# Halves of K stored by token and head, halves of P stored by head: the order of the fp16 stationary operands in SBUF

## The chip, the cores and the metric

The kernel runs on one core of a Trainium2 chip. The metric is the device time of one execution in microseconds; lower is better. Of three runs of the kernel before, the median is 1122.11 us (1119.1 to 1122.72). The profile comes from one further execution.

## The reference

Three stages follow one another in one launch, on 4 batches × 768 tokens with 8 heads of 48.

```python
# 1. delta-rule attention: a 48x48 state for each batch and head, 768 tokens in sequence
k_n = k / (np.linalg.norm(k, axis=-1, keepdims=True) + 1e-06)
for t in range(S):
    y[:, :, t] = np.einsum('bhd,bhde->bhe', q[:, :, t], state)
    v_old = np.einsum('bhde,bhd->bhe', state, kt)
    state = state + bt[:, :, :, None] * np.einsum('bhd,bhe->bhde', kt, vt - v_old)
# 2. mixture of 8 experts (384 -> 1024 -> 384), each token goes to the expert of its largest gate logit
h = np.maximum(x[mask] @ w1[e], 0.0)
out[mask] = gate_w[mask, None] * eom[mask, e, None] * (h @ w2[e])
# 3. gated layer on all 3072 tokens (384 -> 1536 -> 384)
gate = 1.0 / (1.0 + np.exp(-(x @ w_gate)))
return (gate * (x @ w_val)) @ w_out
```

## The kernel before, in words

**Attention.** The 768 tokens are cut into 24 chunks of 32 (`NSTEP`). The recurrence within a chunk is solved at once: a triangular 32×32 system for every batch and head is inverted on VectorE ahead of time, for groups of four chunks. The 4 batches stand in four strips of 32 tokens on the 128 partitions; two batches share the 128 columns of a state matmul. The loop `for s in range(NSTEP)` does one chunk a pass. Its PE stream, in order, with the names that the profile shows:

- `KS`: the keys times the state (fp32). VectorE makes `W` from it: the values less what the state already holds.
- `Y` from `QB`: the queries times the state (fp32).
- `U`: the inverted system `TBD` times `W` (fp32). ScalarE rounds the result to fp16, `UH[:, 0]`, and VectorE stores what is left over as `UH[:, 1]`.
- `XTP`, and later `GL`: the gate of the mixture for the chunk before; then six of eight heads of `GP`, the key-key and key-query products of the chunk 11 ahead, which feed the inverse (`G`) and the masked query-key weights (`P`).
- `Sps` from `KBD`: the state's update. For each half p of the partitions (two batches), three passes over eight heads, 48 matmuls: hi·hi, lo·hi, hi·lo (`PASS`). The stationary operand is `KBD`, 64 rows × 128 columns, and the moving one is `UH`, 48 columns. ScalarE copies the sums to `SH`, with which the next chunk's `KS` starts.
- `Y` from `PBD`: the output within the chunk, 24 matmuls, 128 rows × 128 columns stationary, 48 columns moving.
- `GL`, then the other two heads of `GP`.

`KBD` and `PBD` hold fp16 halves: the upper half is the value rounded to fp16, the lower half the rest, rounded. They are block-diagonal by batch: where a strip's rows meet another batch's columns there are zeros, written once at the start. Each has two buffers, used in turn for pairs of chunks (u = s // 2).

**How K's halves arise.** The raw keys of a pair of chunks are loaded token by token, in the order (d, h) in a row (`load_kth`). ScalarE scales them head by head by the inverse norm (`kh_mul`), then casts them to fp16 (`kh_split_hi`). GpSimd forms the lower half (`kh_split_lo`). Four DMAs on the SP queue (`kexp`) write the strips into `KBD`. In `KBD` a row holds, for each of its two batches, 64 places for d with the 8 heads innermost, so a head's 128 columns are every eighth element.

**How P's halves arise.** `gp_evac` takes the `GP` products out of PSUM with two ScalarE copies, `G` as it lies and `P` turned from (h, i) to (i, h), i being the query's token. GpSimd scales and masks it (`p_split`), ScalarE casts the upper half (`p_split_hi`), GpSimd forms the lower (`p_split_lo`), and four DMAs on the SP queue (`expand`) write the strips into `PBD`. There a row holds, for four batches, 32 tokens with 16 (chunk, head) places innermost, so that a matmul's 128 columns are every sixteenth element. For the first four chunks `p_first` and `p_evac` do the same with a scaled ScalarE copy for each head.

**What sets the order.** Every engine of the attention issues in the order in which the code is written (`Queue` chains each instruction to the one before on its engine). The `Filler` puts the operations of the inverse between VectorE's main ones by a budget of estimated times, when the program is built. So the order doesn't follow measured times. Matmuls on zeros (`zf`, named by the tile they write) fill places where PE would wait.

Ahead of the loop, the first loads, the first inverse and the products of chunks 0 to 11 are made. The experts (lines around 1093 and 1130) and the gated layer (lines 1419 and 1445) follow the loop; during its last four passes the first expert weights are loaded and split.

Of the kernel before, what the change touches and what calls it, by code (L numbers as in the profile page):

```python
# [7 lines left out]
F32 = mybir.dt.float32  # L8
F32R = mybir.dt.float32r
F16 = mybir.dt.float16  # L10
I32 = mybir.dt.int32
U32 = mybir.dt.uint32
AF = mybir.ActivationFunctionType
ALU = mybir.AluOpType
# [134 lines left out]
class Attention:  # L149
# [5 lines left out]
    def run(self, small, acc, zero_fill, small_loads):  # L155
        tc, a, beside = self.tc, self.a, self.beside
        nc = tc.nc
        V, A, G = [Queue(tc, e) for e in (nc.vector, nc.scalar, nc.gpsimd)]
        T, SP = Queue(tc, nc.tensor), Queue(tc, nc.sync)
        engines = (V, A, G, T, SP)  # L160
        ctx, early = ExitStack(), ExitStack()
        wk = ctx.enter_context(tc.tile_pool(name="at_w", bufs=1, side="right"))
        cp = ctx.enter_context(tc.tile_pool(name="at_c", bufs=1, side="right"))
# [9 lines left out]
        rnt = cp.tile([128, NG, 32], F32, name="rnt")  # L173
        nt = cp.tile([128, NG, 32], F32, name="nt")
        mask = cp.tile([128, 32], F32, name="mask")
# [2 lines left out]
        KB = [(ep if i < 8 else cp).tile([128, 2, 64, 8], F32, name=f"KB{i}") for i in range(RK)]  # L178
        QB = [cp.tile([128, 2, 64, 8], F32, name=f"QB{i}") for i in range(2)]
        TBD = [(cp if i else ep).tile([128, 2, 1024], F32, name=f"TBD{i}") for i in range(2)]  # L180
        PBD = [cp.tile([128, 2, 4, 512], F16, name=f"PBD{i}") for i in range(2)]
        KBD = [cp.tile([128, 2, 2, 2, 64, 8], F16, name=f"KBD{i}") for i in range(2)]
        Sps = [pp.tile([128, 512], F32, name=f"Sps{i}") for i in range(2)]
        KT, VT, KTOK, KHG, GPM, PHL, LT = {}, {}, {}, {}, {}, {}, {}

# [19 lines left out]
        def load_v(u):  # L205
            t = wk.tile([128, 2, 384], F32, tag="VT", name="VT", bufs=2)
            SP.dma_start(out=t, in_=a["vtok"][:, 2 * u : 2 * u + 2])
            VT[u] = t
# [36 lines left out]
        QF, PM, PP = {}, {}, {}  # L245
# [6 lines left out]
        def p_first(s):  # L252

            u, s2 = divmod(s, 2)
            q = QF[s]
            if s2 == 0:
                PM[u] = wk.tile([128, 32, 16], F32, tag="PHL", name="PM", bufs=4)
            tag = ("GP", "XTP", "GL", "U")[s]
            ps = pool(tag).tile([128, 8, 64], F32, tag=tag, name="P0", bufs=1)
            for h in range(8):  # L260
                for p in range(2):
                    T.matmul(out=ps[64 * p : 64 * p + 64, h, 0:32], lhsT=KB[s][0:112, p, :, h], rhs=q[0:112, p, :, h], start=True, stop=True)
            PP[s] = ps

        def p_evac(s):
            u, s2 = divmod(s, 2)
            ps = PP.pop(s)
            for h in range(8):
                A.activation(out=PM[u][:, :, 8 * s2 + h], in_=ps[:, h, 0:32], func=AF.Copy, scale=rnt[:, 0, 8 * s + h : 8 * s + h + 1])

        def gp_evac(s):

            ps = GPS.pop(s)
            KT.pop(s)
            g, s4 = divmod(s, 4)
            if s4 == 0 and g > 0:
                GPM[g] = [ep.tile([128, 32, 32], F32, tag=n, name=n, bufs=b) for n, b in (("G", 2), ("P", 2))]
            A.copy(out=GPM[g][0][:, 8 * s4 : 8 * s4 + 8], in_=ps[:, :, 0:32])
            return A.copy(out=GPM[g][1][:, :, 8 * s4 : 8 * s4 + 8].rearrange("p i h -> p h i"), in_=ps[:, :, 32:64]).ins


        PMS = {}
# [1 line left out]
        def p_split(u):  # L284
            g, i = divmod(u, 2)
            if g:
                pm = GPM[g][1][:, :, 16 * i : 16 * i + 16]
                G.tensor_tensor(out=pm, in0=pm, in1=rnt[:, g, 16 * i : 16 * i + 16].unsqueeze(1).to_broadcast([128, 32, 16]), op=ALU.mult)
            else:
                pm = PM.pop(u)  # L290
            G.tensor_tensor(out=pm, in0=pm, in1=mask.unsqueeze(2).to_broadcast([128, 32, 16]), op=ALU.mult)
            PHL[u] = wk.tile([128, 2, 32, 16], F16, tag="PHL", name="PHL", bufs=4)
            PMS[u] = pm

        def p_split_hi(u):
# [4 lines left out]

        def expand(dst, src):
            for b in range(4):
                SP.dma_start(out=dst[32 * b : 32 * b + 32, :, b], in_=src[32 * b : 32 * b + 32].rearrange("p a i k -> p a (i k)"))


        def kh_mul(u, half=None):
            r = rnt[:, u // 2].rearrange("p (s h) -> p s h", s=4)
            for i in (range(2) if half is None else (half,)):
                kt = KTOK[u][:, i]
                if u == 0 or KA:  # L310
                    for h in range(8):
                        A.activation(out=kt[:, :, h], in_=kt[:, :, h], func=AF.Copy, scale=r[:, 2 * (u % 2) + i, h : h + 1])
                    continue
                G.tensor_tensor(out=kt, in0=kt, in1=r[:, 2 * (u % 2) + i].unsqueeze(1).to_broadcast([128, 48, 8]), op=ALU.mult)

        def kh_split_hi(u):
            KH = wk.tile([128, 2, 2, 384], F16, tag="KH", name="KH", bufs=1)
            src = KTOK[u].rearrange("p s d h -> p s (d h)")
            for s in range(2):
                A.copy(out=KH[:, s, 0], in_=src[:, s])  # L320
            KHG[u] = KH

        def kh_split_lo(u):
            KH = KHG[u]
            src = KTOK.pop(u).rearrange("p s d h -> p s (d h)")
            for s in range(2):
                G.tensor_tensor(out=KH[:, s, 1], in0=src[:, s], in1=KH[:, s, 0], op=ALU.subtract)

        def kexp(u):
            KH = KHG.pop(u)  # L330
            for b in range(4):
                SP.dma_start(
                    out=KBD[u % 2][32 * b : 32 * b + 32, :, :, b % 2, 0:48].rearrange("p s a d h -> p (s a) (d h)"),
                    in_=KH[32 * b : 32 * b + 32].rearrange("p s a x -> p (s a) x"))


        def prep(g):
# [257 lines left out]
        def zap(E, t, n=1):  # L595
            d = " ".join("abcdef"[: len(t.shape) - 1])
            t = t.rearrange(f"p {d} -> p ({d})")
            w = t.shape[1] // n
            for i in range(n):
                r = t[:, i * w : (i + 1) * w]  # L600
                ins = A.memzero(r) if E is A else E.memset(r, 0.0)
            return ins.ins

        def zap_off(E, t):

            for par in range(2):
                r = t[64 * par : 64 * par + 64, :, 32 - 32 * par : 64 - 32 * par].rearrange("p a t h -> p a (t h)")
                E.memzero(r) if E is A else E.memset(r, 0.0)
# [43 lines left out]
        zero0()  # L652
        zap(G, KBD[0], 2)
        zap_off(G, KB[6])
        zap_off(G, KB[7])
        zap_off(A, KB[5])
        zap(A, PBD[0], 2)
        zap_off(G, QB[0])
        zap_off(G, QB[1])
        zap_off(G, KB[8])  # L660
        zap(G, PBD[1], 2)
        for i in range(9, RK):
            zap_off(G, KB[i])
        G.tensor_copy(out=lt, in_=small["tri"])
        zap(A, KBD[1], 2)
        zap(A, TBD[1], 2)
# [56 lines left out]
        for f in other0[Q3:]:  # L723
            f()
        expand(PBD[0], PHL.pop(0))
        load_v(1)
# [27 lines left out]
        mm = lambda **kw: T.matmul(skip_group_check=True, **kw)  # L754
# [3 lines left out]
        for s in range(NSTEP):  # L758
            g, s4 = divmod(s, 4)
            u, s2 = divmod(s, 2)  # L760
# [17 lines left out]
            UH = wk.tile([128, 2, 8, 48], F16, tag="UH", name="UH", bufs=2)  # L778
# [16 lines left out]
            if s2 == 0 and 0 < s < NSTEP - 2:  # L795
                expand(PBD[(u + 1) % 2], PHL.pop(u + 1))
                if half:
# [3 lines left out]
            Yp = pp.tile([128, 8, 48], F32, tag="Y", name="Y")  # L801
# [50 lines left out]
            if not last:  # L852
                SH = wk.tile([128, 2, 384], F32, tag="SH", name="SH", bufs=2)
                for p, i in ((0, 0), (0, 1), (0, 2), (1, 0), (1, 1), (1, 2)) if s < LS or not SP2 else ((0, 0), (0, 1), (1, 0), (1, 1), (0, 2), (1, 2)):
                    l, r = PASS[i]
                    if True:
                        for h in range(8):
                            mm(out=Sps[p][:, 48 * h : 48 * h + 48], lhsT=KBD[u % 2][64 * p : 64 * p + 64, s2, l].rearrange("p a d h -> p (a d h)")[:, h::8], rhs=UH[64 * p : 64 * p + 64, r, h], start=False, stop=False)
                    if i == 2:
                        A.copy(out=SH[:, p], in_=Sps[p][:, 0:384])  # L860
            for _ in range(BP.get(s, NP)):
# [1 line left out]

            for i, (l, r) in enumerate(PASS):
                for h in range(8):
                    mm(out=Yp[:, h], lhsT=PBD[u % 2][:, l].rearrange("p b k -> p (b k)")[:, 8 * s2 + h :: 16], rhs=UH[:, r, h], start=(s == 0 and h == 0 and i == 0), stop=(i == 2))
            if s >= 6 and s4 == 2:
                fil.flush(v2)
            if 6 <= s < NSTEP - 2:
# [27 lines left out]
            if s == 0:  # L897
                expand(PBD[1], PHL.pop(1))
                kh_mul(2, 0)
# [632 lines left out]
```

## Time and profile before

| what | value |
|---|---|
| median of three runs | 1122.11 us |
| profiled execution: its time | 1119.2 us |
| profiled execution: its span | 1117.5 us |
| mean granted TensorE clock | 0.862 |
| busy PE / weight loads / VectorE / ScalarE / GpSimd | 1086.5 / 986.8 / 552.1 / 412.5 / 422.4 us |
| first and last KBD matmul | 66.0 and 377.9 us |
| first and last PBD matmul | 70.3 and 391.2 us |

PE is counted busy from a matmul's issue to its modelled end, so that matmuls that overlap in the pipeline leave no gap; PEld counts the weight loads in the same way. The busy time of a group divided by its count is therefore nearer to the distance between two of its matmuls than the mean length of one is. The lines of the page are told apart by the names of the tiles; most of the attention stands under line 95, the helper that records each operation. The granted clock is a share of full speed.

### The profile page before, as it was taken

How to read it: one execution, taken by the hardware profiler on the slowest of the kernel's cores; microseconds unless marked ns; L12 is line 12 of the kernel's file. 1: busy time of each engine (PE TensorE's matmuls, PEld its weight loads, DVE VectorE, ACT ScalarE, POOL GpSimd, SP SyncE). 2: the span in 40 equal slices, each digit the busy share in tenths (PEclk: the TensorE clock that was granted, in tenths of full speed). 3: DMA queues.
4: the chain of work that ended last, by engine and by line, in shares of the span. 5: the costliest groups of instructions: out<-in, count | busy, mean ns of one | idle time of the engine just before them, and what ended most of it. 6: DMA issues, size and time to landing. Idle time of an engine off the chain costs nothing. (4 is left out here: it accounts for less than half of the span.)

```text
span 1117.5 us, 22890 instructions
## 1 busy us (share of the span) xinstructions
PE 1086.5 (97%) x9287; PEld 986.8 (88%) x9288; DVE 552.1 (49%) x1376; ACT 412.5 (37%) x892; POOL 422.4 (38%) x460
## 2 busy tenths in 40 slices
PE   9899999999999999999989999999999999999997
PEld 8798999999999998888888988888888888888886
DVE  7977677877873357756767255430210201201111
ACT  6644545445444245454445422221211211211111
POOL 8544445544642123535544413432131221312312
PEclk8885556755556589999999999999999999999999
DMA  7986634432334336545553322100000000000000
GB/s 188 235 209 158 156 103 129 116 100 75 89 91 137 94 104 217 154 144 185 160 167 110 110 45 71 57 29 1 1 29 1 13 17 1 29 1 1 29 1 28
DMA packets 73535, 100.13 MB, mean 90 GB/s; under 512 B 9721, under 2 KB 62914, under 8 KB 73426
## 3 DMA queue, kind: packets, MB, share of 16 engines
q1 hardware_dynamic: 70354, 89.17, 29.1%
q0 software_dynamic: 3072, 9.46, 2.3%
q8 instruction: 74, 1.21, 0.5%
q14 instruction: 35, 0.29, 0.1%
HBM read 74.94 MB, written 15.80 MB: 81 GB/s over the span
## 5 line engine op out<-in xcount | busy, mean ns | idle before, releaser
L1453 DVE TENSOR_TENSOR gf<-gf,g 128x512 f32<-128x512 f32 x72 | 49.5, 688 | 308.7 <-PE g L1445 308.2
L954 POOL TENSOR_TENSOR gsl<-gf,gsh 128x512 fp32r<-128x512 f32 x68 | 88.4, 1301 | 268.0 <-ACT gsh L953 268.0
L1452 ACT ACTIVATE gf<-g 128x512 f32<-128x512 f32 x72 | 43.0, 597 | 183.4 <-PE g L1445 182.9
L953 ACT CAST gsh<-gf 128x512 fp32r<-128x512 f32 x69 | 42.8, 620 | 146.4 <-DVE gf L1453 146.0
L95 DVE TENSOR_TENSOR X<-X,tmp 128x60 f32<-128x60 f32 (+25 forms) x282 | 91.3, 349 | 1.2
L95 DVE TENSOR_TENSOR tmp<-X,Lt 128x60 f32<-128x60 f32 (+25 forms) x282 | 87.0, 335 | 1.9
L1419 PE MATMUL o<-woh,gsl 128*128 128x384 f32 x272 | 87.2, 338 | 0.0
L1419 PE MATMUL o<-wol,gsh 128*128 128x384 f32 x272 | 86.5, 337 | 0.0
L95 PE MATMUL Sps<-UH,KBD 64*128 64x48 f16 x1104 | 65.4, 228 | 2.6 <-DVE UH L95 2.6
L95 PEld LDWEIGHTS <-KBD 64*128 64x128 f16 x1104 | 62.7, 166 | 5.9 <-issue 4.2
L1134 DVE SCALAR_TENSOR_TENSOR hl<-h,hh 128x460 fp32r<-128x460 f32 (+7 forms) x57 | 33.1, 581 | 65.4 <-ACT hh L1133 65.1
L1445 PE MATMUL g<-yl,wgh 128*128 128x512 f32 x216 | 62.6, 395 | 0.0
L1093 PE MATMUL y<-hh,w2h 128*128 128x460 f32 (+6 forms) x168 | 61.0, 363 | 1.5 <-ACT hh L1133 1.4
L1445 PE MATMUL g<-yl,wvh 128*128 128x512 f32 x216 | 62.3, 395 | 0.0
L1419 PE MATMUL o<-woh,gsh 128*128 128x384 f32 x272 | 61.7, 337 | 0.0
L1445 PE MATMUL g<-yh,wgh 128*128 128x512 f32 x180 | 60.9, 395 | 0.0
L1093 PE MATMUL y<-hh,w2l 128*128 128x460 f32 (+6 forms) x168 | 58.9, 351 | 0.0
L95 ACT ACTIVATE kth<-kth,rnt 128x48 f32<-128x48 f32 x192 | 54.7, 375 | 6.6 <-DMA kth<-in_ktok_dram 6.4
L1419 PEld LDWEIGHTS o<-woh,gsh 128*128 128x128 f32 x272 | 49.7, 188 | 5.8
L95 PE MATMUL GP<-KT,KB 112*64 112x64 f32 x640 | 47.7, 315 | 5.8 <-DMA KB<-in_st_dram 3.7
L1071 POOL TENSOR_TENSOR w1l<-w1r,w1h 128x768 fp32r<-128x768 f32 x19 | 37.1, 1952 | 41.5 <-ACT w1h L1066 41.2
L1419 PEld LDWEIGHTS o<-wol,gsh 128*128 128x128 f32 x272 | 50.6, 188 | 2.4
(333 smaller groups left out, 2559.5 us busy)
## 6 DMA issues: line engine op xcount, KB each, us to landing
w1r<-in_w_dram SPq DMA_DIRECT2D x32, 384.0 KB
w2r<-in_w_dram SPq DMA_DIRECT2D x32, 384.0 KB
KT<-in_st_dram SPq DMA_DIRECT2D x20, 448.0 KB
disp<-TBD SPq DMA_DIRECT2D x8, 772.0 KB
kth<-in_ktok_dram SPq DMA_DIRECT2D x12, 384.0 KB
VT<-in_vtok_dram SPq DMA_DIRECT2D x12, 384.0 KB
KBD<-KH SPq DMA_DIRECT2D x48, 96.0 KB
XG<-in_m2g_dram SPq DMA_DIRECT2D x12, 384.0 KB
```

What stands on the lines that cost most here:

```text
L95: r = f(*args, **kw)
L953: (act or nc.scalar).copy(out=hi, in_=src)
L954: eng.tensor_tensor(out=lo, in0=src, in1=hi, op=ALU.subtract)
L1071: engine.tensor_tensor(out=l, in0=self.raw[b][i], in1=h, op=ALU.subtract)
L1093: self.T.matmul(out=ys[c][:, 0:n], lhsT=w2[l][:, f % 2, 128 * c : 128 * c + 128], rhs=(hh, hl)[r], start=(f == 0 and i == 0), stop=(f == 7 ...
L1134: self.V.scalar_tensor_tensor(out=hl, in0=hp[:, 0:n], scalar=0.0, in1=hh, op0=ALU.max, op1=ALU.subtract)
L1419: T.matmul(out=ops_[m][:, 0:384], lhsT=gh[l][:, 128 * m : 128 * m + 128], rhs=wo[r][:, f], start=(f == 0 and i == 0), stop=(f == 11 and i ...
L1445: T.matmul(out=ps, lhsT=gv[w][l][:, c, 128 * f : 128 * f + 128], rhs=Y[r][c], start=(i == 0 and c == 0), stop=(i == 2 and c == 2))
L1452: A.activation(out=gf, in_=gps[0], func=AF.Sigmoid)
L1453: V.tensor_tensor(out=gf, in0=gf, in1=gps[1], op=ALU.mult)
```

## The change

The axes of four tiles change places, and with them the accesses that write and read them. K's halves `KH` are written in the order (h, d) instead of (d, h): the cast and the subtraction read the fp32 keys through `by_head`, which swaps the two. `KBD` then holds a head's two batches of 64 places next to each other. `P`, its halves `PHL` and `PBD` have the head ahead of the token: (h, i) instead of (i, h), and in `PBD` the four batches of 32 tokens of a head lie next to each other. The 128 columns of each KBD and PBD load are then neighbours in memory.

The DMAs of `kexp` and `expand` write the same bytes, in runs of 48 and 32 elements where they were 384 and 512 long.

```diff
-        PBD = [cp.tile([128, 2, 4, 512], F16, name=f"PBD{i}") for i in range(2)]
-        KBD = [cp.tile([128, 2, 2, 2, 64, 8], F16, name=f"KBD{i}") for i in range(2)]
+        PBD = [cp.tile([128, 2, 16, 4, 32], F16, name=f"PBD{i}") for i in range(2)]
+        KBD = [cp.tile([128, 2, 2, 8, 2, 64], F16, name=f"KBD{i}") for i in range(2)]
...
# p_first, p_evac
-                PM[u] = wk.tile([128, 32, 16], F32, tag="PHL", name="PM", bufs=4)
+                PM[u] = wk.tile([128, 16, 32], F32, tag="PHL", name="PM", bufs=4)
...
-                A.activation(out=PM[u][:, :, 8 * s2 + h], in_=ps[:, h, 0:32], func=AF.Copy, scale=rnt[:, 0, 8 * s + h : 8 * s + h + 1])
+                A.activation(out=PM[u][:, 8 * s2 + h], in_=ps[:, h, 0:32], func=AF.Copy, scale=rnt[:, 0, 8 * s + h : 8 * s + h + 1])
...
# gp_evac
-            return A.copy(out=GPM[g][1][:, :, 8 * s4 : 8 * s4 + 8].rearrange("p i h -> p h i"), in_=ps[:, :, 32:64]).ins
+            return A.copy(out=GPM[g][1][:, 8 * s4 : 8 * s4 + 8], in_=ps[:, :, 32:64]).ins
...
# p_split
-                pm = GPM[g][1][:, :, 16 * i : 16 * i + 16]
-                G.tensor_tensor(out=pm, in0=pm, in1=rnt[:, g, 16 * i : 16 * i + 16].unsqueeze(1).to_broadcast([128, 32, 16]), op=ALU.mult)
+                pm = GPM[g][1][:, 16 * i : 16 * i + 16]
+                G.tensor_tensor(out=pm, in0=pm, in1=rnt[:, g, 16 * i : 16 * i + 16].unsqueeze(2).to_broadcast([128, 16, 32]), op=ALU.mult)
...
-            G.tensor_tensor(out=pm, in0=pm, in1=mask.unsqueeze(2).to_broadcast([128, 32, 16]), op=ALU.mult)
-            PHL[u] = wk.tile([128, 2, 32, 16], F16, tag="PHL", name="PHL", bufs=4)
+            G.tensor_tensor(out=pm, in0=pm, in1=mask.unsqueeze(1).to_broadcast([128, 16, 32]), op=ALU.mult)
+            PHL[u] = wk.tile([128, 2, 16, 32], F16, tag="PHL", name="PHL", bufs=4)
...
# expand
-                SP.dma_start(out=dst[32 * b : 32 * b + 32, :, b], in_=src[32 * b : 32 * b + 32].rearrange("p a i k -> p a (i k)"))
+                SP.dma_start(out=dst[32 * b : 32 * b + 32, :, :, b].rearrange("p a k i -> p (a k) i"), in_=src[32 * b : 32 * b + 32].rearrange("p a k i -> p (a k) i"))
...
+        by_head = lambda x: x.rearrange("p d h -> p h d")
...
# kh_split_hi, kh_split_lo
-            KH = wk.tile([128, 2, 2, 384], F16, tag="KH", name="KH", bufs=1)
+            KH = wk.tile([128, 2, 2, 8, 48], F16, tag="KH", name="KH", bufs=1)
...
-                A.copy(out=KH[:, s, 0], in_=src[:, s])
+                A.copy(out=KH[:, s, 0], in_=by_head(KTOK[u][:, s]))
...
-                G.tensor_tensor(out=KH[:, s, 1], in0=src[:, s], in1=KH[:, s, 0], op=ALU.subtract)
+                G.tensor_tensor(out=KH[:, s, 1], in0=by_head(src[:, s]), in1=KH[:, s, 0], op=ALU.subtract)
...
# kexp
-                    out=KBD[u % 2][32 * b : 32 * b + 32, :, :, b % 2, 0:48].rearrange("p s a d h -> p (s a) (d h)"),
-                    in_=KH[32 * b : 32 * b + 32].rearrange("p s a x -> p (s a) x"))
+                    out=KBD[u % 2][32 * b : 32 * b + 32, :, :, :, b % 2, 0:48].rearrange("p s a h d -> p (s a h) d"),
+                    in_=KH[32 * b : 32 * b + 32].rearrange("p s a h d -> p (s a h) d"))
...
# the loop: Sps and Y
-                            mm(out=Sps[p][:, 48 * h : 48 * h + 48], lhsT=KBD[u % 2][64 * p : 64 * p + 64, s2, l].rearrange("p a d h -> p (a d h)")[:, h::8], rhs=UH[64 * p : 64 * p + 64, r, h], start=False, stop=False)
+                            mm(out=Sps[p][:, 48 * h : 48 * h + 48], lhsT=KBD[u % 2][64 * p : 64 * p + 64, s2, l, h].rearrange("p b d -> p (b d)"), rhs=UH[64 * p : 64 * p + 64, r, h], start=False, stop=False)
...
-                    mm(out=Yp[:, h], lhsT=PBD[u % 2][:, l].rearrange("p b k -> p (b k)")[:, 8 * s2 + h :: 16], rhs=UH[:, r, h], start=(s == 0 and h == 0 and i == 0), stop=(i == 2))
+                    mm(out=Yp[:, h], lhsT=PBD[u % 2][:, l, 8 * s2 + h].rearrange("p b i -> p (b i)"), rhs=UH[:, r, h], start=(s == 0 and h == 0 and i == 0), stop=(i == 2))
```

More of the change, by code (lines that the diff above doesn't have):

```diff
@@ L314, in kh_mul @@
                 G.tensor_tensor(out=kt, in0=kt, in1=r[:, 2 * (u % 2) + i].unsqueeze(1).to_broadcast([128, 48, 8]), op=ALU.mult)
+        by_head = lambda x: x.rearrange("p d h -> p h d")
         def kh_split_hi(u):
-            KH = wk.tile([128, 2, 2, 384], F16, tag="KH", name="KH", bufs=1)
-            src = KTOK[u].rearrange("p s d h -> p s (d h)")
+            KH = wk.tile([128, 2, 2, 8, 48], F16, tag="KH", name="KH", bufs=1)
             for s in range(2):
-                A.copy(out=KH[:, s, 0], in_=src[:, s])
+                A.copy(out=KH[:, s, 0], in_=by_head(KTOK[u][:, s]))
             KHG[u] = KH
         def kh_split_lo(u):
-            KH = KHG[u]
-            src = KTOK.pop(u).rearrange("p s d h -> p s (d h)")
+            KH, src = KHG[u], KTOK.pop(u)
             for s in range(2):
-                G.tensor_tensor(out=KH[:, s, 1], in0=src[:, s], in1=KH[:, s, 0], op=ALU.subtract)
+                G.tensor_tensor(out=KH[:, s, 1], in0=by_head(src[:, s]), in1=KH[:, s, 0], op=ALU.subtract)
         def kexp(u):
```

## The prediction

> **What bounds the kernel now.** I read the page first, then the busy time by stretch, the PE and weight-load timelines of single steps, the waits, and last the DMA queue.
>
> ```profile
> span 1117.5 us, 22890 instructions
> ...
> PEclk8885556755556589999999999999999999999999
> ...
> DMA packets 73535, 100.13 MB, mean 90 GB/s; under 512 B 9721, under 2 KB 62914, under 8 KB 73426
> ...
> q1 hardware_dynamic: 70354, 89.17, 29.1%
> q0 software_dynamic: 3072, 9.46, 2.3%
> ```
>
> The granted clock is low where the attention recurrence runs (slices 3 to 14, 28 us each) and 0.9 or more later. The stretches there, with their columns: stretch, length, busy PE, weight load, DVE, ACT, POOL; clock; DMA share; GB/s:
>
> ```profile
> 40.00:48.00 8.00, 6.49 (x88) 6.19 (x89) 8.00 (x29) 1.62 (x8) 5.64 (x15) 0.79 1.06 267
> ```
> ```profile
> 72.00:392.00 320.00, 316.14 (x4746) 296.66 (x4743) 220.73 (x718) 145.97 (x373) 137.28 (x196) 0.57 0.44 118
> ...
> 72.00:142.00 70.00, 67.40 (x1011) 63.16 (x1008) 50.69 (x168) 34.82 (x86) 25.76 (x33) 0.57 0.65 165
> 142.00:258.00 116.00, 115.11 (x1752) 108.69 (x1748) 89.50 (x279) 56.66 (x146) 60.65 (x86) 0.60 0.43 115
> 258.00:364.00 106.00, 105.63 (x1580) 99.25 (x1579) 70.43 (x230) 46.39 (x121) 45.68 (x69) 0.54 0.35 96
> ```
> ```profile
> 133.14:162.70 29.56, 29.56 (x447) 27.65 (x446) 21.31 (x67) 14.64 (x38) 10.04 (x9) 0.50 0.45 111
> ```
>
> From 72 to 392 us PE has work for 316 of 320 us and DVE for 221. The clock's 0.57 is half clock for 86% of the time, if only 0.5 and 1.0 are granted. So what leaves PE's stream shortens the loop, until DVE comes last. One step of PE, inside the last stretch, which is all at half clock:
>
> ```profile
> 148.12 2.10 PE L95 MATMUL KS<-SH,KB 128*64 128x48 f32 x32
> ...
> 157.07 2.90 PE L95 MATMUL Sps<-UH,KBD 64*128 64x48 f16 x48
> 159.91 1.68 PE L95 MATMUL Y<-UH,PBD 128*128 128x48 f16 x24
> 161.51 0.83 PE L95 MATMUL GL<-wgo,xt 128*64 128x16 f32 x12
> ...
> 162.70 2.10 PE L95 MATMUL KS<-SH,KB 128*64 128x48 f32 x32
> ```
>
> A step takes 162.70 − 148.12 = 14.6 us; the two touched groups are 161.51 − 157.07 = 4.4 of them. KBD's pairs of load and matmul go 2.84 us / 48 = 59 ns apart.
>
> **What columns side by side are worth.** The loads and two groups with which to compare them:
>
> ```profile
> 144.93 1.58 PEld L95 LDWEIGHTS <-PBD 128*128 128x128 f16 x24
> ...
> 147.33 0.20 PEld L95 LDWEIGHTS <-ones 128*128 128x128 f16 x4
> ```
> ```profile
> 256.85 1.27 PE L95 MATMUL GP<-zf 128*128 128x128 f16 x10
> ```
> ```profile
> L95 PEld LDWEIGHTS <-KBD 64*128 64x128 f16 x1104 | 62.7, 166 | 5.9 <-issue 4.2
> ...
> L95 PEld LDWEIGHTS <-PBD 128*128 128x128 f16 x576 | 37.8, 164 | 1.1
> ...
> L95 PEld LDWEIGHTS <-ones 128*128 128x128 f16 x25 | 1.4, 109 | 0.1
> ```
> ```profile
> L95 PE MATMUL GP<-zf 128*128 128x128 f16 x70 | 9.4, 307 | 0.0
> ```
>
> PBD's pairs go (1.58 − 0.164) / 23 = 62 ns apart. The operand "ones" is also fp16 with 128 columns, but they lie side by side: its load takes 109 ns against 166 and 164, and four of them go (0.20 − 0.109) / 3 = 30 ns apart, in the stretch at half clock, ahead of matmuls of 8 to 32 columns. The zf matmuls, 128 columns each, go (1.27 − 0.307) / 9 = 107 ns apart in a part of the loop at half clock, 0.83 ns a column; the 48 columns of a KBD or PBD matmul are thus 40 ns, and 20 at full clock. Now the load is the longer half of the pair. After the change the pair goes at the longer of 30 and 40 ns at half clock, of 30 and 20 at full: 0.86 × 40 + 0.14 × 30 = 38.6 ns. The ends are 30 (all at full clock) and 59 to 62 (no effect); I take 38.6, as "ones" and zf are of this stage.
>
> Gain on PE: 48 × (59 − 38.6) = 0.98 us in each of 23 steps (the last has no KBD group) and 24 × (62 − 38.6) = 0.56 in each of 24: 22.5 + 13.5 = 36.0 us, 1.5 a step.
>
> The Trainium skill (TensorE: Matmul & The Clock Gate, Weight-path perf modes) says that fast weight load is on whenever 128 columns of a type other than fp32 are loaded, for column steps from −1,023 to 1,024 elements, packed or strided. By that rule alone KBD and PBD have it already and the gain is 0; the rows of "ones" and KBD differ by 57 ns all the same.
>
> **What takes some of it back: DVE.** W (DVE) follows the KS group and opens the U group; the second half of UH (DVE) opens the third pass of KBD, its 17th pair. Between them DVE works through a fixed list of the inverse's columns.
>
> ```profile
> DVE W L95 <- PE KS L95: 28.8, 13, 3.6
> ```
> ```profile
> 99.37 1.88 PE L95 MATMUL Sps<-UH,KBD 64*128 64x48 f16 x32 [2.60 <-DVE UH L95]
> ```
> ```profile
> 166.03 0.54 DVE L95 SCALAR_TENSOR_TENSOR W<-VT,KS 128x384 f32<-128x384 f32 x1
> ```
> ```profile
> 167.19 2.01 PE L95 MATMUL U<-W,TBD 64*64 64x48 f32 x32
> ```
> ```profile
> 225.04 2.02 PE L95 MATMUL U<-W,TBD 64*64 64x48 f32 x32 [0.89 <-DVE W L95]
> ```
> ```profile
> 285.42 2.79 PE L95 MATMUL Sps<-UH,KBD 64*128 64x48 f16 x46
> ```
> ```profile
> 285.78 0.55 DVE L95 TENSOR_TENSOR UH<-U,UH 128x384 f16<-128x384 f32 x1
> ```
>
> In 13 of 23 steps DVE waits before W, 28.8 / 13 = 2.2 us on average, more than the 1.5 that PE gains; and a W that is late is covered by Y's matmuls, which stand between KS and U. Four places lack that cover. At 99 us PE waits for UH already: the gain of the 16 pairs ahead, 16 × 20 ns = 0.3 us, is lost. At 166 W ends 0.6 us before U: 1.5 − 0.6 = 0.9 lost. At 225 PE waits for W already: 1.5 lost. At 285 UH ends at 286.33 and the 17th pair stands at 285.42 + 16 × 0.06 = 286.4: 1.5 lost. Sum 4.2 us; next late is U, behind W.
>
> ACT is no third bound, since it waits for PE all through the loop:
>
> ```profile
> ACT SH L95 <- PE Sps L95: 72.3, 40, 5.5
> ACT UH L95 <- PE U L95: 49.4, 22, 4.5
> ```
> ```profile
> L95 ACT COPY P<-GP 128x256 f32<-128x256 f32 x16 | 10.4, 649 | 1.9 <-POOL PHL L95 1.9
> L95 ACT CAST KH<-kth 128x384 f16<-128x384 f32 x22 | 10.0, 502 | 0.0
> ...
> L95 ACT COPY G<-GP 128x256 f32<-128x256 f32 x16 | 6.0, 375 | 6.3 <-PE GP L95 6.3
> ```
>
> P's eviction, now without a stride, comes down from 649 towards G's 375 ns. KH's cast, which now reads with one, stays at 502 or rises by the same ratio to 870 ns, twice in two steps. That is at most 0.74 − 2 × 0.27 = 0.2 us more in two steps, behind UH's wait of 49.4 / 22 = 2.2 us in nearly every step; without that wait UH's first half would be late by all of it. POOL's P and KH operations keep their sizes; POOL works 137 of 320 us, and what it hands on is read 30 us later (below), so a dearer stride there costs nothing.
>
> **The DMAs.** The expansions write runs of 48 and 32 fp16 (96 and 64 B) where 768 and 1,024 B stood: 4,096 packets in place of 512 for each KBD, 4,096 in place of 256 for each PBD, 12 times each, so 98,304 for 9,216.
>
> ```profile
> 40.59 4.88 SPq L95 DMA_DIRECT2D KBD<-KH x4
> ...
> 46.15 1.32 SPq L95 DMA_DIRECT2D KB<-in_st_dram x2
> ```
> ```profile
> 52.56 2.24 PE L95 MATMUL GP<-KT,KB 112*64 112x64 f32 x32 [3.48 <-DMA KB<-in_st_dram]
> ```
> ```profile
> 213.15 2.65 SPq L95 DMA_DIRECT2D KBD<-KH x4
> ```
> ```profile
> 244.08 2.12 PE L95 MATMUL Sps<-UH,KBD 64*128 64x48 f16 x35
> ```
>
> No row prices a short packet. Queue 1 gives 0.291 × 16 engines × 1117.5 us / 70,354 = 74 ns at 1,267 B, queue 0 gives 0.023 × 16 × 1117.5 / 3,072 = 134 ns at 3,080 B. By bytes alone 80 B are 5 ns; by a line through both, 32 + 0.033 a byte, 35 ns; at worst a whole mean packet, 74. I take 20, the middle of the two that allow for size, and keep 5 and 74 as ends. In the loop two steps then load each engine with 512 × 20 ns = 10.2 us, where 48 × 74 = 3.6 stood. Two steps will be 26 us for 29.2; the room is 26 − (0.65 × 29.2 − 3.6) = 10.6 us from 72 to 142, 17.0 to 258 (share 0.43), 19.4 after (0.35). A KBD issued at 213 is read at 244. So it hides, only just early on; past that room KB and QB come late, and with them PE. Ahead of the loop nothing hides it: the share is 1.06, and KB's load, for which PE waits at 52.56, stands behind KBD's four DMAs on SP's queue: 256 × 20 − 32 × 74 ns = +2.7 us (−1.1 to +16.6).
>
> The Trainium skill (DMA: Bandwidth & Descriptors, Measured) gives a floor of about 10.5 ns a packet; by it this term would be 0.3 us, an estimate.
>
> **Sum.** −36.0 + 4.2 + 2.7 = −29.1 us. The profiled execution took 1119.2 us, 2.9 below the median of 1122.1 and near the lower end of the runs; 1119.2 − 29.1 = 1090. What follows the loop only starts earlier, and no instruction changes its place in any engine's order.
>
> **Rivals.**
> - *The clock rises.* The same matmuls in shorter steps leave PE's array less idle, and PE may hold 1.0 as it does later; against it, 0.50 was granted from 133 to 163 with PE busy all through. The pairs then go at 30 ns: 1,104 × 29 + 576 × 32 ns = 50.4 us; DVE's losses double to 8, the 2.7 stay: 1079. Four to fourteen zf matmuls a step at half their 107 ns may add 0.5 us in 24 steps: 1067.
> - *Short packets are dear: slower.* Place: the DMA engines. At p ns a packet the loss is 0.256p − 2.4 ahead of the loop and what 0.512p has over the rooms, 10.6 in 2 pairs of steps, 17.0 in 4, 19.4 in 4. It eats the 31.8 us left after DVE at p = 37; at 45 it is 9.1 + 24.8 + 24.2 + 14.6 = 73 and the time 1160. For it: the line's 35 lies close. Against it: both queues' packets came mostly from memory outside the core, these don't. From 25 to 37 ns the time is 1096 to 1119.
> - *The load gets no faster*, as the skill's rule above has it, or since KBD's 64 rows make it 166 ns. PBD, with all 128 rows, has 164, against the second; "ones" against both, though its four loads are of one operand. Time: 1119.2 + 2.7 = 1122.
>
> **Chances.** Forecast 0.58 (its own range 1080 to 1100: 5 to 30 ns a packet, DVE's loss up to twice as large, some more clock), clock 0.16 (1067 to 1080), packets of 25 to 37 ns 0.11 (1096 to 1117), no faster load 0.07, dear packets 0.08. The time is the forecast's, 1090. The range 1068 to 1112 leaves out the last two and the outer ends of the two before. About 0.3%, 3.4 us, is what a measurement of this kernel can tell from no change: faster 0.85, same 0.07, slower 0.08.
>
> **What would show it.** Loads of KBD and PBD near 109 ns, their pairs near 40 ns apart, steps of 13 us; DMA packets near 162,600, of them under 512 B near 108,000; PE's wait for KB ahead of the loop 2 to 3 us longer; more waits of PE for W and UH, none for SH. I am wrong if the loads stay at 166 ns, or if PE waits for KB, QB, KBD or PBD inside the loop.

## The result and the profile after

The median of the changed kernel is 1084.08 us (four runs, 1081.01 to 1087.11) against 1121.09 for the kernel before on the same chip: a ratio of 0.967, 95% interval 0.963 to 0.971. A second series beside other kernels gave 1080.30 us (six runs, 1076.33 to 1082.32) against 1119.19, 0.965 (0.962 to 0.967). The profiled execution took 1081.45 us, against 1119.2 before. The page, as before:

```profile
span 1079.7 us, 22890 instructions
PEclk9886558958589899999999999999999999999999
DMA  7999876744475364556534132000000000000000
DMA packets 162623, 100.13 MB, mean 93 GB/s; under 512 B 108025, under 2 KB 152002, under 8 KB 162514
q1 hardware_dynamic: 159442, 89.17, 35.5%
```

As many instructions and bytes as before, and 89,088 more packets. The clock row has more nines and eights in slices 3 to 12, where the recurrence runs (27 us a slice), and the DMA row reads 7 to 9 in slices 1 to 6. The weight loads by group (count | busy us, mean ns):

```profile
L95 PEld LDWEIGHTS <-KBD 64*128 64x128 f16 x1104 | 33.9, 103 | 5.4 <-issue 3.3
L95 PEld LDWEIGHTS <-PBD 128*128 128x128 f16 x576 | 20.3, 107 | 1.2
L95 PEld LDWEIGHTS <-ones 128*128 128x128 f16 x25 | 1.3, 102 | 0.4 <-issue 0.4
```

KBD and PBD now load like "ones". Two stretches of PE's timeline, one at half clock and one at full:

```profile
126.16 1.95 PE L95 MATMUL Sps<-UH,KBD 64*128 64x48 f16 x48
128.05 1.14 PE L95 MATMUL Y<-UH,PBD 128*128 128x48 f16 x24
...
303.46 1.30 PE L95 MATMUL Sps<-UH,KBD 64*128 64x48 f16 x48
304.70 0.78 PE L95 MATMUL Y<-UH,PBD 128*128 128x48 f16 x24
```

At half clock one matmul of either group lasts 0.21 us, so KBD's 48 go (1.95 − 0.21) / 47 = 37 ns apart and PBD's 24 go (1.14 − 0.21) / 23 = 40; at full clock, with 0.18 us for one, 24 and 26 ns. The windows of the loop (columns as in the prediction):

```profile
72.00:142.00 70.00, 62.81 (x1072) 58.07 (x1072) 56.86 (x176) 36.10 (x87) 28.65 (x35) 0.59 0.94 179
142.00:258.00 116.00, 111.59 (x2029) 104.92 (x2026) 106.39 (x317) 67.82 (x173) 70.95 (x97) 0.75 0.64 123
```

DVE is busy 106.4 of 116 us where it was 89.5: it has become nearly as full as PE. PE's waits, longest first (total us, times, longest):

```profile
PE U L95 <- DVE W L95: 11.5, 5, 4.3
PE GP L95 <- DMA KB<-in_st_dram: 8.6, 2, 7.6
...
PE Sps L95 <- DVE UH L95: 2.4, 2, 1.3
PE Y L95 <- DMA QB<-in_st_dram: 1.8, 1, 1.8
```

From the first KS of step 1 to that of step 23 the loop took 307.7 us before (72.63 to 380.34) and takes 271.2 now (71.80 to 343.01): 36.5 of the 37.8 us by which the span is shorter. The start is 0.8 us earlier, and what follows is 0.5 shorter.

### The profile page after: what moved, and what is told of

Same layout as the page of the kernel before. It is cut to its first block, busy times and chain, and to the rows that moved or that the text cites. A ratio compares the mean times of both kernels' runs of the same rounds, so it can differ in the third digit from the quotient of the medians.

```text
span 1079.7 us, 22890 instructions
## 1 busy us (share of the span) xinstructions
PE 1034.0 (96%) x9287; PEld 935.4 (87%) x9288; DVE 568.3 (53%) x1376; ACT 417.5 (39%) x892; POOL 428.4 (40%) x460
## 5 line engine op out<-in xcount | busy, mean ns | idle before, releaser
L95 DVE TENSOR_TENSOR X<-X,tmp 128x60 f32<-128x60 f32 (+25 forms) x282 | 98.0, 373 | 1.2
L95 DVE TENSOR_TENSOR tmp<-X,Lt 128x60 f32<-128x60 f32 (+25 forms) x282 | 94.2, 360 | 1.9
L95 PE MATMUL U<-W,TBD 64*64 64x48 f32 x768 | 47.8, 290 | 11.5 <-DVE W L95 11.5
L95 PEld LDWEIGHTS U<-W,TBD 64*64 64x64 f32 x768 | 44.4, 200 | 15.3 <-DVE W L95 12.5
L95 PEld LDWEIGHTS GP<-KT,KB 112*64 112x64 f32 x640 | 42.5, 220 | 14.7 <-POOL KH L95 7.7
```

The lines of the kernel that those rows point to most:

```text
L95: r = f(*args, **kw)
```

## The experiments

**One side alone.** Only K's halves, or only P's, are stored by head; the other side keeps its old layout.

```diff
# only K; the other kernel takes KBD from before and PBD from the change
-        PBD = [cp.tile([128, 2, 16, 4, 32], F16, name=f"PBD{i}") for i in range(2)]
+        PBD = [cp.tile([128, 2, 4, 512], F16, name=f"PBD{i}") for i in range(2)]
```

> Only K's halves and KBD change; P's halves and PBD stay as before. Theory: the distance of the columns in memory sets the load's time, tile by tile. KBD's loads come down to 93 to 119 ns and its group in the loop from 63.6 to 36 to 41 us (by the clock), PBD's loads stay at 164 ns and its group at 35; VectorE's late W and UH cost PE 5 to 10 us; 1098 to 1103 us. Rival, that the gain of the whole change came through the granted clock (0.57 before, 0.71 after in the loop) and not from the loads: KBD's pairs come down, but without a higher clock no more than 20 us are gained on them, and the time stays above 1105.

> Only P, its halves and PBD change; K's halves and KBD stay as before. Theory (column distance): PBD's loads at 96 to 119 ns and its group from 35.4 to 20 to 23 us, KBD's unchanged at 166 ns; KB's load ahead of the loop isn't held up by KBD's short packets, so PE's wait for it stays at 3.5 us; 1102 to 1107 us. Rival, that 64 active rows and not the column distance make KBD's loads slow and PBD gains by something else: KBD's loads would come down here too, or PBD's pairs stay near 62 ns.

Measured: K alone 1099.08 us, ratio 0.985 (0.981 to 0.989); P alone 1105.51 us, 0.988 (0.984 to 0.993). The loads, of K alone and then of P alone:

```profile
L95 PEld LDWEIGHTS <-PBD 128*128 128x128 f16 x576 | 37.7, 163 | 1.2
L95 PEld LDWEIGHTS <-KBD 64*128 64x128 f16 x1104 | 35.3, 105 | 10.9 <-issue 9.2
```
```profile
L95 PEld LDWEIGHTS <-KBD 64*128 64x128 f16 x1104 | 62.8, 166 | 6.2 <-issue 4.5
L95 PEld LDWEIGHTS <-PBD 128*128 128x128 f16 x576 | 23.6, 116 | 1.0
```

Each side speeds up its own loads and leaves the other's, whether 64 rows are loaded or 128. So the layout does it, on both sides. The loop is 285.6 us with K alone and 296.2 with P alone, −22.1 and −11.5, in sum −33.6; the change takes 36.5 us off the loop in its first execution and 33.2 in that of its second series, so the two gains add up within what two executions differ by. With K alone PE waits 7.5 us for UH. Ahead of the loop, where the change waits 7.6 us for KB, it waits 5.6; the profile puts that down to GpSimd's lower half of K, but the group that waits reads KT and KB alone and starts at 55.46, as late as with the change (55.25). With P alone the wait there was 5.5 us; I had expected 3.5.

**How near must the columns be?** Two heads, then four, are interleaved, so that a load's columns lie 4 or 8 bytes apart. The transfers come in runs two or four times as long, with half or a quarter of the short packets.

```diff
-        KBD = [cp.tile([128, 2, 2, 8, 2, 64], F16, name=f"KBD{i}") for i in range(2)]
+        KBD = [cp.tile([128, 2, 2, 4, 2, 64, 2], F16, name=f"KBD{i}") for i in range(2)]
...
-  lhsT=KBD[u % 2][64 * p : 64 * p + 64, s2, l, h].rearrange("p b d -> p (b d)")
+  lhsT=KBD[u % 2][64 * p : 64 * p + 64, s2, l, h // 2].rearrange("p b d j -> p (b d j)")[:, h % 2 :: 2]
```

> The same change, but with two heads interleaved in KBD and PBD, so that a load's 128 columns are every second fp16 element; the DMAs' runs are twice as long (192 and 128 B) and half as many. Theory that two neighbouring fp16 must be read at once to gain: loads near 166 ns and pairs 59 to 62 ns apart as before, time 1118 to 1122. Rival that a wider line of SBUF is read and only far columns are slow: loads between 100 and 140 ns, pairs 40 ns at half clock, time 1080 to 1090, with PE's wait for KB ahead of the loop shorter than the 7.6 us of the changed kernel.

> Four heads interleaved in KBD and PBD: a load's columns are every fourth fp16 element (8 B apart; they were 16 and 32 B apart before, 4 B in the kernel with two heads); the expansion's packets are a quarter of the changed kernel's, 24,576. If the load's cost grows with the span that its columns cover: loads of 125 to 135 ns, pairs 30 ns apart at full clock where 25 stood. If it depends on whether a line of 8 B or more serves several columns: loads 93 to 119 ns as with side-by-side columns, pairs at 25 and 40 ns, 1072 to 1080 us. If only pairs within 4 B gain: 166 ns, pairs 60 ns apart, 1112 to 1120 us.

Measured: two heads 1076.61 us, ratio 0.963 (0.960 to 0.967); four heads 1081.62 us, 0.968 (0.965 to 0.971). The loads of two heads, then of four:

```profile
L95 PEld LDWEIGHTS <-KBD 64*128 64x128 f16 x1104 | 33.3, 102 | 11.4 <-issue 9.3
L95 PEld LDWEIGHTS <-PBD 128*128 128x128 f16 x576 | 20.2, 108 | 1.1
```
```profile
L95 PEld LDWEIGHTS <-KBD 64*128 64x128 f16 x1104 | 38.0, 114 | 6.6 <-issue 4.6
L95 PEld LDWEIGHTS <-PBD 128*128 128x128 f16 x576 | 22.6, 118 | 1.5 <-issue 0.4
```

The theory that only neighbours gain fell. Columns 4 bytes apart load as fast as neighbours. Those 8 bytes apart take longer at full clock, where a KBD load lasts 114 ns instead of 93; at half clock both last about 114. The median distance of PBD's pairs at full clock was 25 ns at 2 and 4 bytes and 33 at 8; at 32 bytes (K alone, whose PBD is that of before) 62. At half clock it was 40 at 2, 4 and 8 bytes, since there the 48 columns of the matmul are the longer half. So there is no edge between neighbours and the rest: the pace falls off between 4 and 16 bytes (KBD with P alone has 60 ns at 16). At 8 bytes neither theory holds as put: the loads stay under the 125 ns of the first, and the pairs are not at the 25 of the second. The time of four heads is that of the change.

**The price of the packets.** Each expansion is issued twice, the first time into a tile `TW` that nobody reads.

```diff
+        TW = cp.tile([128, 32, 80], F16, name="TW")
...
             for b in range(4):
+                SP.dma_start(out=TW[32 * b : 32 * b + 32, :, 0:32], in_=src[32 * b : 32 * b + 32].rearrange("p a k i -> p (a k) i"))
...
# kexp: the same ahead of each KBD write, from KH into TW[:, :, 32:80]
```

> The changed kernel with every expansion DMA issued twice, the second into a tile that nobody reads: 98,304 short packets more. Theory (short packets of 11 to 14 ns, hidden in the loop): PE's wait for KB ahead of the loop grows from 7.6 to 11 to 14 us, the loop itself stays within 3 us of its 271; 1086 to 1092 us. Rival (the packets load the loop itself, through late KB and QB or by slowing VectorE's accesses): PE waits for KB, QB, KBD or PBD inside the loop, or VectorE's mean times rise again as they did from before to after (349 to 373 ns), and the time is over 1095.

Measured: 1108.45 us, ratio 0.992 (0.990 to 0.995), 24 to 28 us over the two series of the change; the theory that the loop stays as it is fell. The queue, PE's waits and the windows:

```profile
q1 hardware_dynamic: 259282, 97.04, 39.7%
```
```profile
PE Y L95 <- DMA QB<-in_st_dram: 19.5, 4, 6.4
PE GP L95 <- DMA KB<-in_st_dram: 16.6, 5, 11.7
```
```profile
72.00:142.00 70.00, 55.29 (x963) 51.54 (x962) 52.22 (x157) 31.57 (x77) 30.00 (x37) 0.62 0.97 180
142.00:258.00 116.00, 104.17 (x1830) 97.10 (x1828) 95.78 (x293) 61.36 (x155) 58.02 (x83) 0.65 0.90 157
```

With another 98,304 packets the transfer engines stand at 0.97 and 0.90, and PE waits 19.5 us for QB where the change has 1.8. By the page, the added packets took (0.397 × 1101.6 − 0.355 × 1079.7) × 16 = 865 us of engine time, 9 ns each.

The doubling adds issues as well as packets, and no run parts the two. SP is busy issuing for 91% and 86% of the two windows here, for 72% and 53% with the change. Ahead of the longest wait for QB it issues without a gap, and PE is ready at 122.2 us, just before the QB transfers are issued:

```profile
122.38 1.17 SPq L95 DMA_DIRECT2D QB<-in_st_dram  x2
```
```profile
128.62 2.18 PE L95 MATMUL Y<-SH,QB 128*64 128x48 f32 x32 [6.40 <-DMA QB<-in_st_dram]
```

So the full issue queue is as good a reason for the late QB as the full transfer engines.

Does half the number then gain in proportion? Two heads interleaved were timed again beside the change itself.

> The kernel with two heads interleaved again, beside the changed kernel on one chip, to price the packets below the count of the change. It issues 49,152 fewer packets than that; doubling the packets had cost 24 us for 98,304 more. Theory that each packet costs in proportion: 12 us less than the changed kernel, 1072. Rival, that packets only cost where the transfer engines are near full (0.94 in 72-142 us against 0.60-0.64 later): a gain of 0-6 us, 1078-1084.

> The changed kernel itself, for the comparison on the same chip: 1081-1087 us by both theories.

Measured: two heads 1078.92 us, 0.964 (0.962 to 0.967); the change 1080.30 us, 0.965 (0.962 to 0.967). They differ by 1.4 us, within their intervals, not by 12. The packets cost PE nearly nothing at the number that the change has; doubled, where the engines and SP's queue fill, they cost much. The first series' 7 us between the two did not come back, so two heads are not shown to be better than one.

**Can the waits that are left be taken away?** On the kernel with two heads, chunk 10's loads are issued ahead of the first expansion and of the second zero fill; the planner's budgets of VectorE's other work for a step are raised (`TB`, `TC`); both together; and, last, the budgets lowered.

```diff
# early
-        zero_fill(SP, 1, TBD[1])
         load_kth(1)
+        ahead(10)
+        zero_fill(SP, 1, TBD[1])
         kexp(0)
...
-        ahead(10)
...
# budgets: 4.8 and 4.4, later 3.6 and 3.2
-TC = 3.8
+TC = 4.4
-TB = 4.2
+TB = 4.8
```

> The kernel with two heads interleaved, and chunk 10's loads (KT, KB) on SP's queue ahead of the first KBD expansion and the second zero fill. Theory (the first expansion's packets hold up KB's load ahead of the loop): PE's wait for KB falls from 6.5 to under 2.5 us, the loop starts 3 to 5 us earlier, 1071 to 1075 us. Rival (VectorE's list in steps 1 to 3 ends at the same time whatever PE does): the wait goes, and PE waits the more for W and UH in steps 1 and 2; 1075 to 1079.

> The kernel with two heads interleaved, and a larger share of the inverse planned into each step (budget between UH and W 4.8 for 4.2, late 4.4 for 3.8), so that less of it is left for the forced end of each group of four chunks. Theory (W and UH are late where the rest of a group's inverse stands in one step): PE's waits for W and UH in the steps 7, 11 and 15 fall, in sum from 12.5 to 5 to 8 us; 1070 to 1075. Rival (VectorE with GpSimd beside it is the bound over each whole group): the waits move to other steps and the time stays within 3 us of 1077.

> Two heads interleaved with both edits, the earlier loads and the larger budget. Theory: the two gains add, 1065 to 1071. Rival: no more than the better of the two.

> The kernel with two heads interleaved, with smaller budgets of other work per step: TB 3.6 for 4.2, TC 3.2 for 3.8. With larger ones (4.8, 4.4) TensorE's waits for W grew from 4.5 to 17.6 us and those for UH from 8.0 to 14.0, the loop from 267.1 to 283.0 us. Theory that the budget only sets how far VectorE's and ScalarE's share of other work stands ahead of W and UH: the waits fall below 6 us together, the loop to 258-264 us, and some of what leaves the loop comes back behind it: 1071-1078 us. Rival, that the waits come from VectorE being slowed beside GpSimd and not from the amount: waits stay at 10-14 us, and the stretch behind the loop grows by 5-10 us over 741: 1080-1088 us.

Measured: early 1083.12 us, 0.969 (0.966 to 0.971); budgets raised 1093.44 us, 0.977 (0.975 to 0.979); both 1097.49 us, 0.981 (0.979 to 0.982); budgets lowered 1119.34 us, 1.001 (0.999 to 1.003). PE's waits, early, raised, lowered:

```profile
PE U L95 <- DVE W L95: 13.8, 4, 8.2
PE GP L95 <- DMA KB<-in_st_dram: 5.4, 3, 2.8
```
```profile
PE U L95 <- DVE W L95: 17.6, 7, 6.7
PE Sps L95 <- DVE UH L95: 9.2, 5, 4.6
```
```profile
PE U L95 <- DVE W L95: 44.2, 7, 14.4
PE GP L95 <- DMA KB<-in_st_dram: 7.2, 3, 5.6
```

The early loads shorten the longest wait for KB from 6.5 to 2.8 us, and the waits for W and UH together grow from 12.5 to 17.2: what PE gains ahead of the loop, DVE doesn't have. The loop doesn't start sooner either: the first KS of step 1 stands at 71.17 us, against 70.64 and 71.40 in the two executions without the edit. No gain in time is shown. The budgets failed in both directions; both theories on the lowered ones had the time at most at 1088. Raised, more of the inverse stands ahead of each W. Lowered, it is left over for the end of a group of four chunks, since it must be finished before the next group's first U. DVE in step 16 of that kernel, from the end of KS to W:

```profile
L95 DVE TENSOR_TENSOR tmp<-X,Lt 128x80 f32<-128x80 f32 (+9 forms) x19 | 9.3, 518 | 0.1
L95 DVE TENSOR_TENSOR X<-X,tmp 128x80 f32<-128x80 f32 (+9 forms) x20 | 6.3, 348 | 0.1
L95 DVE STREAM_TRANSPOSE XT<-X 128x1024 f32<-128x1024 f32 x1 | 1.9, 1901 | 0.1
```
```profile
289.63 2.02 PE L95 MATMUL U<-W,TBD 64*64 64x48 f32 x32 [14.23 <-DVE W L95]
```

39 operations of the inverse run without a gap while PE waits 14.2 us. Its loads are as fast as the change's, and the whole gain is gone. So DVE's work for a group, and how it is spread over the group's four steps, bounds the loop next.

## Why the prediction was right, and where its terms were off

The time, 1084 us for 1090, is of the right sign and cause, inside the forecast's own range of 1080 to 1100. That the sum came so near is partly luck: the touched groups gained more than forecast and DVE took more back, and the two errors offset each other in part. By terms, from the profiled execution of the change and, behind the slash, that of its second series (span 1080.1 us):

| term | predicted | measured |
|---|---|---|
| KBD and PBD groups, without PE's waits for UH | −36.0 | −42.9 / −37.3 |
| PE's waits for DVE's W, UH and X in the loop (3.5 before) | +4.2 | +10.4 / +6.3 |
| the loop's other groups, the wait for QB among them | 0 | −4.0 / −2.2 |
| ahead of the loop | +2.7 | −0.8 / −1.3 |
| behind it | 0 | −0.5 / −2.9 |
| span | −29.1 | −37.8 / −37.4 |

The measured groups are those of the 22 steps between the two KS; the forecast's −36.0 counts 23 KBD and 24 PBD groups. Over the whole kernel these gained 45.8 and 40.8 us.

- *The pace of a pair* was right at half clock (37 and 40 ns for 40) and too slow at full (24 and 26 for 30): "ones" had four loads in a stretch at half clock, and I carried their 30 ns over. The Trainium skill (TensorE: Matmul & The Clock Gate, Wait — 56ns, not 53.3ns?) has a floor of about 25 ns between matmuls however few columns they have; the rows at full clock agree. Its rule on fast weight load that I weighed (Weight-path perf modes: on for every column step from −1,023 to 1,024 elements) is not borne out as a statement of pace: loads with steps of 8 and 16 elements took 166 and 164 ns, with steps of 1 and 2 from 102 to 116.
- *The clock* was forecast unchanged. It rose: from the granted clock of the trace over the loop, 0.57 before, 0.71 in the first execution of the change, 0.61 in the second. That rival was thus partly true, but most of the gain doesn't rest on it: P alone, at 0.57 over the loop as before, takes 11.5 us off it, and K alone, at 0.61, 22.1. The two executions of the change have spans of 1079.7 and 1080.1 us; at the higher clock the touched groups are 5.6 us shorter and PE's waits for DVE 4.1 longer. Yet the clock isn't without effect: of the four runs of the first series, the two with 0.912 and 0.918 over the whole execution took 1081 us, the two with 0.889 and 0.899 took 1087. What raised it stays open.
- *DVE* takes some back at the four places that I had named, steps 2, 7, 11 and 15, and more of it: 6.3 to 10.4 us for 4.2. In the first execution PE's waits there grew by 1.7, 0.8, 2.7 and 2.8 us (predicted 0.3, 0.9, 1.5 and 1.5); steps 1 and 16 were added with 1.1 and 1.3. In the second they grew by 0.4, 0.6, 1.0 and 1.5, nearly as predicted, and steps 1, 13 and 16 were added with 2.8 together. The rows of step 11 and of step 16:

```profile
212.49 1.99 PE L95 MATMUL U<-W,TBD 64*64 64x48 f32 x32 [3.61 <-DVE W L95]
...
279.76 1.29 PE L95 MATMUL Sps<-UH,KBD 64*128 64x48 f16 x32 [1.29 <-DVE UH L95]
```

What was missed is that DVE itself got slower. Its operations for the inverse over the whole execution, before and after (count | busy us, mean ns):

```profile
L95 DVE TENSOR_TENSOR X<-X,tmp 128x60 f32<-128x60 f32 (+25 forms) x282 | 91.3, 349 | 1.2
L95 DVE TENSOR_TENSOR tmp<-X,Lt 128x60 f32<-128x60 f32 (+25 forms) x282 | 87.0, 335 | 1.9
```
```profile
L95 DVE TENSOR_TENSOR X<-X,tmp 128x60 f32<-128x60 f32 (+25 forms) x282 | 98.0, 373 | 1.2
L95 DVE TENSOR_TENSOR tmp<-X,Lt 128x60 f32<-128x60 f32 (+25 forms) x282 | 94.2, 360 | 1.9
```

From 50 us on they take 376 ns on average for 351, some 12 us in all 474. Those that lie for over 30% of their time beside a GpSimd operation take 535 ns, the others 257 (491 and 262 before); among operations of equal shape the ratio is the same, 2.1, so their sizes don't explain it. The Trainium skill (Advanced Engine Details and Errata, VectorE Performance Modes) says that GpSimd shares VectorE's second port, so that its instructions and VectorE's two-port instructions block each other. Its table gives `tensor_tensor`, which these operations are, no two-port mode; so that sentence doesn't cover them, and no run here shows what slows them beside GpSimd.
- *The 2.7 us ahead of the loop* came as predicted, and by step 2 nothing is left of them. PE's products with KB there start at 55.25 us instead of 52.56 (56.01 in the second execution); the wait itself grew by 4.1 us, since PE came to it 1.4 sooner:

```profile
55.25 2.26 PE L95 MATMUL GP<-KT,KB 112*64 112x64 f32 x32 [7.60 <-DMA KB<-in_st_dram]
```

Yet UH of step 2 is written at the same time in three executions, before, after and after again:

```profile
98.78 0.54 DVE L95 TENSOR_TENSOR UH<-U,UH 128x384 f16<-128x384 f32 x1
```
```profile
98.97 0.54 DVE L95 TENSOR_TENSOR UH<-U,UH 128x384 f16<-128x384 f32 x1
```
```profile
98.88 0.54 DVE L95 TENSOR_TENSOR UH<-U,UH 128x384 f16<-128x384 f32 x1
```

The agreement is in part chance, for DVE gets there in two ways. Its stretch up to there, before and in the second execution of the change (columns: stretch, length, busy DVE; clock; DMA share; GB/s):

```profile
66.50:99.30 32.80, 27.67 (x67) 0.70 0.62 161
```
```profile
66.50:99.30 32.80, 31.07 (x68) 0.65 1.03 194
```

Before, DVE is idle for 5.1 of these 32.8 us, ahead of W and UH; with the change for 1.7 (in the first execution for 0.7), while its operations take longer. So DVE's slack took up the later start of PE, and with the slack gone the first two steps gained nothing, of which I had counted all but 0.3 us. The point isn't fixed by itself: UH of step 2 stands at 97.3 us with two heads, at 95.0 with four and at 103.8 with the expansions doubled. The step of the sum that failed is that the start and the first steps were booked as independent. From that point to step 23's KS the stretch went from 281.6 to 244.0 us, −37.6 (−34.6 in the second): the whole gain.

- *The packets* were priced at 20 ns. The page gives (0.355 × 1079.7 − 0.291 × 1117.5) × 16 = 930 us more engine time; if the 9,216 that went took nothing, that is 9.5 ns a packet, and if they took the 74 ns of the mean packet, 16.4. The packets' own records in the trace give 14 ns on average for 64 as for 96 bytes, and 20 and 18 ahead of the loop, from 30 to 72 us, where my term stands. "Hidden, only just early on" holds: the share is 0.94 from 72 to 142 us, and there stands the only wait for a transfer inside the loop, 1.8 us for QB, 0.9 in the second execution. I had put such waits at nothing and said that one would make me wrong; by that sign the term was too good. It cost no time, since later in the same step PE still waits for DVE, 4.3 us for W and in the second execution 3.0 for UH. The Trainium skill (DMA: Bandwidth & Descriptors, Measured) has about 10.5 ns as a floor for a packet, measured on loads from HBM; the mean of 14 lies above it, but 45% of the 64-byte records show 8 ns or less.
- *ACT and POOL.* P's eviction came down to 380 ns, as expected from G's 375. KH's cast went past the 870 allowed:

```profile
L95 ACT CAST KH<-kth 128x384 f16<-128x384 f32 x24 | 20.4, 899 | 0.0
L95 ACT COPY P<-GP 128x256 f32<-128x256 f32 x20 | 7.6, 380 | 2.6 <-POOL PHL L95 2.6
```

Neither bounds: in the loop ACT waits 61.9 us for U, more than before, and 45.7 for Sps, less.

## What to carry to other kernels

A weight load in fp16 is worth laying out so that its columns are at most 4 bytes apart, wherever the load and not the matmul sets the distance of two pairs; they needn't be neighbours, which leaves room for longer runs in the transfer that writes them. The gain of a shorter step ends where the next engine has no slack left: read that engine's idle time stretch by stretch, since a later start can vanish in it, and a gain can be lost for want of it. Short packets cost next to nothing here while the transfer engines were at most 0.94 busy, so price them by the share of the stretch, and of the queue that issues them, and not by their number alone.

## What the runs showed of the hardware

- The distance of two loads of 128 fp16 columns, each ahead of a matmul of 48, grows with the columns' spacing. At full clock it is 25 ns at 2 and 4 bytes, 33 at 8, 60 at 16 (KBD with P alone) and 62 at 32 (PBD with K alone). At half clock it is 40 at 2, 4 and 8 bytes; at 16 and 32 bytes the clock doesn't matter to it.
- The recorded length of these loads follows the clock, too, at close spacing: KBD's with the change take 93 ns at full clock and 115 at half. With four heads, 8 bytes apart, they take 114 at both, so it isn't shown that the load proper is slower at half clock.
- The granted clock over the same loop differs between executions: 0.57 before, 0.71 and 0.61 in two of the change, 0.57 with P alone. Their spans were 1079.7 and 1080.1 us in the two of the change, while among the four runs of its first series lower clock went with 6 us more.
- An issue of many short packets holds up its queue: the median of one of SP's KBD issues went from 601 to 832 ns, the longest from 2.1 to 3.1 us (with two heads, half the packets, 629 ns and 2.0 us):

```profile
L95 SPq DMA_DIRECT2D KBD<-KH x48: 585/832/3144, 40.5 to 326.1; - x48
```
